# One decode block with its backward pass: K read once, dq from a per-head matrix summed in the forward pass, softmax with keys on partitions, 8 KB rows

## The chip, the cores and the metric

The kernel runs on one core of one Trainium2 chip. The metric is the device time of one execution in microseconds (us), as a median of several executions.

The engines are TensorE (PE; PEld is its weight load), VectorE (DVE), ScalarE (ACT), GpSimd (POOL) and SyncE (SP), each with its own list of instructions, and 16 DMA engines. HBM is the device memory; PSUM is the memory into which the kernel's matmuls write.

## The reference

A decode step: batch 4, one query per sequence, model width 512, 32 heads of 128, 4096 cached keys per head, so 128 pairs of batch and head. The outputs are the step's result and all gradients.

```
q = layernorm(x) @ wq                        # 32 heads of 128
p = softmax(q @ K^T / sqrt(128));  o = p @ V
h = x + o @ wo
h2 = h + (silu(ln(h) @ w1) * (ln(h) @ w3)) @ w2
outputs: h2 and the gradients of x, k_cache, v_cache, wq, wo, w1, w3, w2
```

One cache, K or V, is 134.2 MB in bf16, and so is the gradient of each. Per head, the gradients are two outer products, grad_v = p dO^T and grad_k = dS q^T, with dS = p (dP - c) / sqrt(128), dP = V dO and c = o . dO. The query's gradient is dq = K^T dS.

## The kernel before

It runs the caches in four passes: S = K q and O = V^T p forward; dP = V dO with the grad_v writes; dq = K^T dS with the grad_k writes. So K is read twice and V twice.

```
def load_transposed_half(...):                 # 2048 keys: load, 16 transposes, copies out of PSUM
    dma_eng.dma_start(out=Xh[:], in_=src_rows.rearrange("(p j) d -> p j d", p=P))
    ...
            nc.tensor.transpose(pt[:, i, :], Xh[:, g * GW + i, :], ident_b[:])
        evac_copy(XT[:, g * GW:(g + 1) * GW, :], pt[:], eng=...)
def S_head(b, h, half): ...                    # the query is the weight: all heads' scores in rows
        nc.tensor.matmul(S_ps[QB * b:QB * (b + 1), ...], lhsT=T[...], rhs=KT[...], tile_position=(0, QB * b))
...
for b, h:                                      # last pass: K again
    Kb = kp.tile([P, 2, SJ2, Dh], BF16, ...);  eng.dma_start(out=Kb[:], in_=A_k_cache[b, h]...)
    ... 32 matmuls: dq_ps[...] += T[:, g, ...]^T Kb[:, hh, jj, :]
    nc.vector.tensor_tensor(out=gk[:], in0=dSTall[:, :, bh:bh + 1].to_broadcast([P, SJ, Dh]),
                            in1=rt[:, None, :].to_broadcast([P, SJ, Dh]), op=ALU.mult)
    nc.gpsimd.dma_start(out=out_2[b, h]..., in_=gk...)
...                                            # then, alone at the end: dq transposed, grad of wq, dx
```

## Time and profile before

| | before |
|---|---|
| time, median | 2487.18 us (first 3 runs), 2483.14 us (beside the changed kernel) |
| HBM read / written | 555 / 282 MB |
| forward; MLP; two backward stages; tail | 874; 98; 702 + 718; 48 us |

The main lines stand in the prediction below. One more gives its shape: each place in the row is a fortieth of the span, 62 us, and the digit is the DMA engines' busy share in tenths.

```profile
DMA  9778887888888790799999999997998999999993
```

Read it from left to right: 7 and 8 in the forward stage, a hole at the MLP, 9 through both backward stages, 3 at the tail. The DMA engines bound only the right half. The left half waits for something else.

### The profile page before, as it was taken

How to read it: one execution, taken by the hardware profiler on the slowest of the kernel's cores; microseconds unless marked ns; L12 is line 12 of the kernel's file. 1: busy time of each engine (PE TensorE's matmuls, PEld its weight loads, DVE VectorE, ACT ScalarE, POOL GpSimd, SP SyncE). 2: the span in 40 equal slices, each digit the busy share in tenths (PEclk: the TensorE clock that was granted, in tenths of full speed). 3: DMA queues.
4: the chain of work that ended last, by engine and by line, in shares of the span. 5: the costliest groups of instructions: out<-in, count | busy, mean ns of one | idle time of the engine just before them, and what ended most of it. 6: DMA issues, size and time to landing. Idle time of an engine off the chain costs nothing.

```text
span 2477.8 us, 46386 instructions
## 1 busy us (share of the span) xinstructions
PE 1839.8 (74%) x19974; PEld 1310.2 (53%) x19974; DVE 1503.7 (61%) x1487; ACT 916.8 (37%) x1239; POOL 212.3 (9%) x307
## 2 busy tenths in 40 slices
PE   5999888888888678878777878886655655655655
PEld 3556665655656565455544545553444555554552
DVE  3443323323223104788888898884776888888884
ACT  2443333323233104677776877775321000000001
POOL 1000000000000000111111111111211111111110
PEclk9999999999999897899999999997677777678686
DMA  9778887888888790799999999997998999999993
GB/s 336 233 239 299 329 328 289 336 300 306 298 306 329 288 344 31 307 416 385 386 383 368 391 410 384 386 382 273 382 408 324 401 399 412 398 391 407 415 418 153
DMA packets 222029, 840.47 MB, mean 339 GB/s; under 512 B 17648, under 2 KB 17656, under 8 KB 220800
## 3 DMA queue, kind: packets, MB, share of 16 engines
q1 hardware_dynamic: 92816, 345.87, 37.1%
q0 software_dynamic: 73888, 284.26, 28.3%
q10 hardware_dynamic: 55120, 207.37, 22.8%
q8 instruction: 156, 2.56, 0.4%
q14 instruction: 49, 0.40, 0.0%
HBM read 554.97 MB, written 282.34 MB: 338 GB/s over the span
## 4 chain that ended last, share of the span: by engine, by line
PE 31%; issue 24%; DMA 20%; ACT 17%; DVE 4%; POOL 4%; ACTq 1%; POOLq 0%; DVEq 0%; SPq 0%
ACT XT L155 15%; DMA Vb<-in_A_v_cache_dram 10%; PE pt_tps L205 10%; PE S_ps L285 7%; PE O_ps L351 6%; DMA Xh<-in_A_v_cache_dram 5%; PE dP_ps L630 5%; POOL out_dram L745 3%; DMA Xh<-in_A_k_cache_dram 2%; DMA out_dram<-gk 1%; DVE gk L739 1%; DVE XT L157 1%; PE pt_wT L215 1%; DMA w_sb<-in_B_w_dram 1%; ACTq L200 1%
## 5 line engine op out<-in xcount | busy, mean ns | idle before, releaser
L155 ACT COPY XT<-pt_tps 128x1024 bf16<-128x1024 bf16 x768 | 735.9, 1021 | 694.8 <-PE pt_tps L205 425.3
L205 PE MATMUL pt_tps<-ident_b,Xh 128*128 128x128 bf16 x8192 | 609.5, 221 | 214.0 <-ACT XT L155 91.4
L205 PEld LDWEIGHTS <-Xh 128*128 128x128 bf16 x8192 | 486.2, 98 | 402.5 <-issue 284.5
L739 DVE TENSOR_TENSOR gk<-dSTall,rt 128x4096 bf16<-128x4096 bf16 x128 | 565.9, 4423 | 112.0 <-DMA out_dram<-gk 88.7
L641 DVE TENSOR_TENSOR gv<-PTall,rt 128x4096 bf16<-128x4096 bf16 x128 | 566.3, 4425 | 97.7 <-ACT rt L595 84.8
L729 PE MATMUL dq_ps<-Kb,Tk 128*32 128x128 bf16 x4096 | 365.2, 270 | 220.8 <-DVE Tk L722 220.5
L729 PEld LDWEIGHTS <-Tk 128*32 128x32 bf16 x4096 | 335.4, 124 | 264.1 <-DVE Tk L722 246.7
L351 PE MATMUL O_ps<-Vb,Tp 128*32 128x128 bf16 x4096 | 265.7, 224 | 56.0 <-DMA Vb<-in_A_v_cache_dram 53.0
L157 DVE COPY XT<-pt_tps 128x1024 bf16<-128x1024 bf16 x256 | 177.0, 691 | 188.4 <-PE pt_tps L205 167.4
L285 PE MATMUL S_ps<-XT,Tq 128*32 128x512 bf16 x1024 | 277.9, 386 | 11.2 <-ACT XT L155 9.4
L351 PEld LDWEIGHTS <-Tp 128*32 128x32 bf16 x4096 | 242.5, 100 | 65.1 <-issue 51.1
L595 ACT CAST rt<-rep_ps 128x128 bf16<-128x128 f32 x256 | 73.2, 286 | 536.5 <-DVE gk L739 507.2
L630 PE MATMUL dP_ps<-XT,Td 128*32 128x512 bf16 x1024 | 245.9, 382 | 0.4 <-DVE d_up_rows L157 0.4
L280 DVE COPY Tq<-qT_bf 128x1 bf16<-128x1 bf16 x256 | 39.4, 156 | 274.2 <-PE S_ps L285 273.7
L647 POOL DMA_DIRECT2D out_dram<-gv x128 | 90.3, 706 | 632.8 <-DVE Td L625 550.1
L745 POOL DMA_DIRECT2D out_dram<-gk x128 | 91.6, 716 | 561.2 <-DVE Tk L722 459.9
L630 PEld LDWEIGHTS <-Td 128*32 128x32 bf16 x1024 | 85.9, 96 | 101.3 <-issue 2.1
L285 PEld LDWEIGHTS <-Tq 128*32 128x32 bf16 x1024 | 78.5, 96 | 85.1 <-issue 24.5
L344 DVE COPY Tp<-PTall 128x32 bf16<-128x32 bf16 x128 | 29.3, 242 | 138.4 <-PE O_ps L351 137.4
L432 POOL DMA_DIRECT2D oflat_bf<-O_sb x4 | 2.0, 502 | 805.8 <-ACT O_sb L362 805.8
L593 PEld LDWEIGHTS <-ones_b 1*128 1x128 bf16 x256 | 23.6, 93 | 62.1 <-issue 51.3
L593 PE MATMUL rep_ps<-qflat,ones_b 1*128 1x128 bf16 x128 | 31.9, 249 | 8.7 <-ACT rt L595 8.7
(198 smaller groups left out, 582.4 us busy)
## 6 DMA issues: line engine op xcount, KB each, us to landing
Xh<-in_A_v_cache_dram SPq DMA_DIRECT2D x256, 512.0 KB, 7.0
out_dram<-gv POOLq DMA_DIRECT2D x128, 1024.0 KB, 9.0
out_dram<-gk POOLq DMA_DIRECT2D x128, 1024.0 KB, 10.5
Xh<-in_A_k_cache_dram SPq DMA_DIRECT2D x128, 512.0 KB, 5.9
Vb<-in_A_v_cache_dram ACTq DMA_DIRECT2D x64, 1024.0 KB, 9.0
Vb<-in_A_v_cache_dram SPq DMA_DIRECT2D x64, 1024.0 KB, 9.8
Xh<-in_A_k_cache_dram ACTq DMA_DIRECT2D x128, 512.0 KB, 4.5
Kb<-in_A_k_cache_dram SPq DMA_DIRECT2D x64, 1024.0 KB, 10.0
```

Of the source, the lines that this page charges most:

```text
L155: nc.scalar.copy(out=out_ap, in_=in_ap)
L157: nc.vector.tensor_copy(out=out_ap, in_=in_ap)
L205: nc.tensor.transpose(pt[:, i, :], Xh[:, g * GW + i, :], ident_b[:])
L285: nc.tensor.matmul(S_ps[QB * b:QB * (b + 1), c * SW:(c + 1) * SW], lhsT=T[:, qcol - h:qcol - h + QB], rhs=KT[:, c * SWJ:(c + 1) * SWJ, :], ...
L351: nc.tensor.matmul(O_ps[QB * b:QB * (b + 1), :], lhsT=T[:, g, qcol - h:qcol - h + QB], rhs=Vb[:, hh, jj, :], start=(h == 0 and g == 0), st ...
L595: nc.scalar.copy(out=rt[:], in_=ps[:])
L630: nc.tensor.matmul(dP_ps[QB * b:QB * (b + 1), c * SW:(c + 1) * SW], lhsT=T[:, qcol - h:qcol - h + QB], rhs=VT[:, c * SWJ:(c + 1) * SWJ, :] ...
L641: nc.vector.tensor_tensor(out=gv[:], in0=PTall[:, :, bh:bh + 1].to_broadcast([P, SJ, Dh]), in1=rt[:, None, :].to_broadcast([P, SJ, Dh]), o ...
L647: nc.gpsimd.dma_start(out=out_3[b, h].rearrange("(hh p j) d -> p hh j d", hh=2, p=P), in_=gv.rearrange("p (hh j) d -> p hh j d", hh=2))
L729: nc.tensor.matmul(dq_ps[QB * b:QB * (b + 1), :], lhsT=T[:, g, qcol - h:qcol - h + QB], rhs=Kb[:, hh, jj, :], start=(h == 0 and g == 0), s ...
L739: nc.vector.tensor_tensor(out=gk[:], in0=dSTall[:, :, bh:bh + 1].to_broadcast([P, SJ, Dh]), in1=rt[:, None, :].to_broadcast([P, SJ, Dh]), ...
L745: nc.gpsimd.dma_start(out=out_2[b, h].rearrange("(hh p j) d -> p hh j d", hh=2, p=P), in_=gk.rearrange("p (hh j) d -> p hh j d", hh=2))
```

## The change

Intent: the key dimension stays on the partitions throughout. Then P and dS need no transposing, and forward forms for each head the products PK[k, d] = p[k] K[k, d] and M = sum over k of V[k, :]^T [PK[k, :], p[k]], a 128 x 129 matrix, and kP = sum over k of PK. From these, dq = (M^T dO - c kP) / sqrt(128) without K. The second K pass disappears, one backward loop replaces two, and what stood at the tail moves into that loop. A head's 4096 keys lie 32 to a partition, so rows in DRAM are 8 KB in place of 4 KB. The outer products are written in pairs of elements, so that no operand's innermost step is 0.

The diff, cut to its core:

```
-            nc.tensor.matmul(S_ps[QB * b:QB * (b + 1), ...], lhsT=T[...], rhs=KT[...], ...)
+            for j in range(SJ):
+                nc.tensor.matmul(S_ps[:, hl, j:j + 1], lhsT=KT[:, j, :], rhs=qT_bf[:, bh:bh + 1], start=True, stop=True)
...
+        def softmax(gi):                       # a pair of heads: max, transpose, max, broadcast, exp, sum, 1/sum
+            nc.vector.tensor_reduce(out=mx[:], in_=S_ps[:], axis=AX.X, op=ALU.max)
+            nc.tensor.transpose(xps[0:G, 0:P], mx[:], ident_f[:])
...
+            nc.vector.tensor_tensor(out=P_all[:, gi * G:(gi + 1) * G, :], in0=E[:], in1=rl[...], op=ALU.mult)
+        def M_head(gi, hl):
...
+            nc.vector.tensor_tensor(out=PK[:, :, 0:Dh]..., in0=Kn..., in1=PK[:, :, None, Dh:PKW]..., op=ALU.mult)
+            for j in range(SJ):
+                nc.tensor.matmul(M_ps[:], lhsT=Vn[:, j, :], rhs=PK[:, j, :], start=(j == 0), stop=(j == SJ - 1))
+            for c in range(2):
+                for q in range(4):
+                    nc.tensor.matmul(kP_ps[32 * q:32 * (q + 1), :, :], lhsT=ones_window(w), rhs=PK[:, j0:j0 + 4, 0:Dh], ...)
+            nc.scalar.copy(out=M_all[:, bh, :], in_=M_ps[:, 0:Dh + 1])      # M_all is float32
...
+        for gi in range(NGI + 1):
+            if gi < NGI:
+                for hl in range(G):
+                    S_head(gi, hl)
+                softmax(gi)
+            if gi > 0:
+                for hl in range(G):
+                    M_head(gi - 1, hl)
...
-    (the loop over K that made dq)
+                    nc.tensor.matmul(st_dq["ps"][:, bh:bh + 1], lhsT=M_all[:, bh, 0:Dh], rhs=dOT_f[:, bh:bh + 1], ...)
+            nc.vector.tensor_tensor(out=gv.rearrange("p j (r t) -> p j r t", t=2), in0=P2[...], in1=rdo[...], op=ALU.mult)
+            nc.gpsimd.dma_start(out=rows_of(out_3[b, h]), in_=gv[:])
...
+            nc.vector.tensor_tensor(out=gk.rearrange("p j (r t) -> p j r t", t=2), in0=dS2[...], in1=rq[...], op=ALU.mult)
+            nc.gpsimd.dma_start(out=rows_of(out_2[b, h]), in_=gk[:])
```

## The prediction

The sum came to 833 + 85 + 1052 + 10 = 1980 us, and 1970 was said; the last 10 rested on rates of loads and stores. Two terms of the sum are estimates: 400 GB/s for a saturated mix (the two backward stages of the kernel before had 384 and 388; of the 11 whole fortieths of the last one, ten had 382 to 418), and 2.3 us for each of PK, gv and gk (gv and gk took 4.42 us before). So are the 0.7, 0.4 and 0.8 us for kP, for softmax's small products and for VectorE's small operations. Rival 1 says that the three would cost 4.42 us.

> **What bounds the kernel now.** I read first the table of stretches, cut at the kernel's own stage borders (found in the timeline), then the costliest groups, then the DMA queues, and last the timeline for the price of single instructions.
>
> ```profile
> core 0: us, PE busy (x) PEld busy (x) DVE busy (x) ACT busy (x) POOL busy (x), PEclk, DMA share, GB/s
> 0.00:38.00 38.00, 12.37 (x203) 11.29 (x204) 10.96 (x20) 6.30 (x9) 7.59 (x16) 1.00 0.97 366
> 38.00:912.00 874.00, 739.77 (x9213) 534.19 (x9211) 271.51 (x685) 278.21 (x289) 1.50 (x3) 0.97 0.82 302
> 912.00:1010.00 98.00, 76.41 (x832) 48.92 (x832) 33.86 (x96) 33.67 (x66) 2.02 (x6) 0.74 0.26 92
> 1010.00:1712.00 702.00, 560.69 (x5277) 349.48 (x5277) 587.23 (x390) 508.68 (x641) 93.89 (x130) 0.99 0.99 384
> 1712.00:2430.00 718.00, 426.33 (x4392) 359.57 (x4390) 584.07 (x268) 80.55 (x219) 104.59 (x147) 0.73 0.98 388
> 2430.00:2478.00 48.00, 24.25 (x65) 6.78 (x65) 16.12 (x30) 9.38 (x16) 2.72 (x5) 0.61 0.28 110
> ```
>
> The rows are: start; forward attention (S and O); the MLP and its backward; dP with the grad_v writes; dq with the grad_k writes; tail. The last two columns decide. The two backward stages hold the DMA engines at 98 to 99%: 1420 us are set by **bytes**. The forward stage has a DMA share of 0.82 and 302 GB/s, with PE the busiest engine: it is set by PE's **order and hand-overs** (transpose, copy out of PSUM, matmul). The 98 us of the MLP and the 48 us of the tail are chains of dependent work with the DMA nearly idle.
>
> ```profile
> L155 ACT COPY XT<-pt_tps 128x1024 bf16<-128x1024 bf16 x768 | 735.9, 1021 | 694.8 <-PE pt_tps L205 425.3
> L739 DVE TENSOR_TENSOR gk<-dSTall,rt 128x4096 bf16<-128x4096 bf16 x128 | 565.9, 4423 | 112.0 <-DMA out_dram<-gk 88.7
> L641 DVE TENSOR_TENSOR gv<-PTall,rt 128x4096 bf16<-128x4096 bf16 x128 | 566.3, 4425 | 97.7 <-ACT rt L595 84.8
> L157 DVE COPY XT<-pt_tps 128x1024 bf16<-128x1024 bf16 x256 | 177.0, 691 | 188.4 <-PE pt_tps L205 167.4
> ```
>
> These are the prices of the large elementwise work: 4.42 us for an outer product, 1.02 us (ACT) or 0.69 us (DVE) for a copy of eight transposes. With DVE at 4.42 us in each of two stages, those stages sit just under the DMA bound (587 of 702 us, 584 of 718 us).
>
> ```profile
> q1 hardware_dynamic: 92816, 345.87, 37.1%
> q0 software_dynamic: 73888, 284.26, 28.3%
> q10 hardware_dynamic: 55120, 207.37, 22.8%
> HBM read 554.97 MB, written 282.34 MB: 338 GB/s over the span
> ```
>
> Loads (q1, q10): 345.87 MB in 37.1% of 2477.8 us is 376 GB/s, and q10 gives 367; the stores (q0) give 405. One K or V pass is 134.2 MB: four are read, two written.
>
> ```profile
> 32.20 3.47 PE L228 MATMUL qT_ps<-xhatT,wq_sb 128*128 128x4 bf16 x125 [0.24 <-DVE xhatT L157]
> 409.02 0.38 PE L285 MATMUL S_ps<-XT,Tq 128*32 128x512 bf16 x1
> 409.02 0.39 PE L351 MATMUL O_ps<-Vb,Tp 128*32 128x128 bf16 x4
> 409.24 0.38 PE L285 MATMUL S_ps<-XT,Tq 128*32 128x512 bf16 x1
> ```
>
> The first line: 125 matmuls with full 128x128 weights and four columns in 3.47 us, 28 ns each. The others: S matmuls start 0.22 us apart although four O matmuls for another column group lie between them, so those cost nothing extra.
>
> [...]
>
> **The change part by part.**
>
> *Bytes.* The second K pass goes (-134.2 MB); wo is read once more (+4.2). Left: 425 read + 282 written = 707 MB. Rows grow from 4 KB to 8 KB. A 4 KB packet on a load queue took 16 x 4096 B / 372 GB/s = 176 ns[...]. I use 400 for a saturated mix[...].
>
> *Forward, per head.* Removed: 8 S matmuls of 512 columns (8 x 0.216 = 1.73 us; spacing above), window copies. Kept: 32 transposes (eight in 0.45 us, 56 ns each: 1.8 us). Added: 32 S matmuls of one column (32 x 28 ns = 0.9 us), 32 M matmuls of 130 columns in place of the O ones (about 57 ns: 1.8 us), 8 kP matmuls of 512 columns on four column groups (two rounds of 0.216 together, 1.7 us one by one; the built order breaks them into pieces, so I take 0.7), and softmax's small fp32 matmuls (0.4). Sum: PE 5.6 us a head; before it was 1.8 + 1.73 + 1.8 = 5.3. ACT: 3 copies x 1.02 + exp, M copy: some 3.7. DVE: PK = K*P over 4096 elements written as repeated pairs: [...] 2.3 us[...]; + 0.69 + some 0.8 of small operations = 3.8. DMA: 2.1 MB at 400 GB/s = 5.2. PE and DMA lie close, so the period is PE's work plus hand-overs. In the old steady part (S of a batch beside O of the one before: 96 heads between 196 and 823 us) a head took 6.5 us for 5.3 of work. The new loop has fuller buffers of PE work (S, M and kP of two groups are interleaved in the built order, softmax's steps have 6 to 20 M matmuls between them), so I take **6.2 us**. 128 x 6.2 = 794, + 33 start (wq first; the DMA prefetches meanwhile) + 6 drain = **833 us**, against 912. The old last 90 us, O alone for a batch, are absorbed.
>
> *MLP.* The output projection now accumulates in the forward loop (-7 us, the old attn matmuls), dhh moves ahead; loads of w1 to w3 still start only when forward memory is free. I take **85 us** for 98.
>
> *Backward.* One loop replaces two and the dS transposes between. Per head: 3 MB, 3.146 MB / 400 = 7.9 us. Beside it DVE: gv + gk at 2.3 each + 0.4 = 5.0 us; ACT: 4 copies at 0.94 spacing + replicas 0.3 = 4.1; PE: 1.8 + 0.9 + little = 3. All hidden. With the small gradients and wq, 420.7 MB / 400 = **1052 us**, against 1420.
>
> *Tail.* dq is a matrix product per head with the P-K-V sums, done in the first heads of backward, and dx and grad_wq become jobs inside the loop: 48 us become some **10** of drain.
>
> Sum: 833 + 85 + 1052 + 10 = 1980; I say **1970**[...].
>
> **The rivals.**
> 1. *DVE becomes the bound.* [...] PK, gv and gk cost 4.42 us. Backward would need 2 x 4.42 + 0.4 = 9.3 us a head, 1190 us plus jobs; forward DVE 6.0, about as long as PE. Total some 2150. [...] Chance 1 in 10.
> 2. *Hand-overs of softmax.* S, max, transpose, max, broadcast, exp, sum, reciprocal cross engines about eight times per two heads. If PE stands still for 2 us each time, forward is 7.2 us a head, 960 us, total 2100. For: the old stage lost 1.2 us a head on simpler hand-overs. Against: the interleaving.
> 3. *Buffers too few.* gv and gk have two buffers each; a store landed 9.0 to 10.5 us after issue, plus 2.3 us of filling and about 1 of waiting: 14 us against 15.8 for two heads. It just fits; if landing grows to 14, backward gets 8.5 us a head, +80 us.
> 4. *All better.* Forward DMA-bound: 277 MB / 400 = 692, total 1840.
>
> **Range and chances.** Rivals 1 and 2 give the top, 4 the bottom: 1850 to 2090. Even rivals 1 and 2 together (some 2250) stay under 2487 - 50. Faster 0.97, within 2% 0.02, slower 0.01.
>
> **What would show it.** HBM read about 425 MB. gv, gk, PK at 2.3 us (4.4 would be rival 1). DMA share 0.97 or more in backward at 395 to 410 GB/s; if DVE is busy over 90% there, or its waits for the stores' landing are large, rivals 1 or 3. Forward DMA share about 0.85 at 330 GB/s, PE over 85% busy; PE waiting for nm, exp or mx by over 100 us in total would be rival 2. No stretch of idle DMA at the end. The prediction is wrong if 8 KB rows run below 385 GB/s or forward takes longer than 912 us.

## The result, and the profile after

The changed kernel takes **2204.57 us** (2201.46 to 2205.61, 4 runs), the one before 2483.14 beside it. The ratio is 0.8876 (95% interval 0.8849 to 0.8904). Ratios here are the mean time of one kernel's fast runs over that of the other's of the same rounds, so not quite the ratio of the medians. The direction was right. The time is 235 us above the 1970 predicted and outside the range.

The table of stretches of the kernel after, cut at its own stage borders; the columns are those of the prediction's table. The rows are start, forward, MLP, dq, backward loop, and what is left to store after the last dP.

```profile
0.00:38.00 38.00, 22.86 (x398) 21.20 (x399) 11.94 (x28) 15.53 (x22) 2.68 (x15) 0.93 0.89 360
38.00:944.00 906.00, 791.59 (x13424) 650.62 (x13421) 478.70 (x791) 441.74 (x756) 0.44 (x2) 0.98 0.74 293
944.00:1023.00 79.00, 55.76 (x660) 40.04 (x657) 24.70 (x67) 25.07 (x39) 0.00 (x0) 0.65 0.38 124
1023.00:1086.00 63.00, 62.70 (x328) 61.38 (x325) 7.38 (x10) 5.20 (x8) 2.65 (x5) 0.50 0.19 69
1086.00:2127.00 1041.00, 670.13 (x8695) 548.25 (x8695) 584.73 (x510) 586.00 (x697) 189.22 (x376) 0.59 0.95 376
2127.00:2202.00 75.00, 0.58 (x4) 0.31 (x3) 49.09 (x30) 1.17 (x2) 17.72 (x35) 0.50 0.84 345
```

Set it against the prediction's sum. Forward ends at 944 us where 833 was predicted (+111). The MLP takes 79 (85 predicted, -6). Then come 63 us that the sum doesn't have: TensorE is busy all the time, at half clock, with the DMA engines nearly idle. The backward loop with its end takes 1116 us, where 1052 and 10 were predicted (+54). That makes +222 on the sum of 1980.

The queues and three groups of the kernel after (a group is line, engine, operation, tiles, shapes, count; then busy us and mean ns of one; then the idle time ahead of it and what ended it):

```profile
q1 hardware_dynamic: 66512, 418.94, 49.1%
q0 software_dynamic: 40704, 282.43, 31.5%
HBM read 424.94 MB, written 282.34 MB: 321 GB/s over the span
...
L679 DVE TENSOR_TENSOR gk<-dS,rq 128x4096 bf16<-128x4096 bf16 x128 | 293.2, 2290 | 381.5 <-DMA out_dram<-gk 377.4
L665 DVE TENSOR_TENSOR gv<-P,rdo 128x4096 bf16<-128x4096 bf16 x128 | 292.2, 2283 | 6.9 <-DMA out_dram<-gv 4.7
L288 DVE TENSOR_TENSOR PK<-Kn,PK 128x4096 bf16<-128x4096 bf16 x128 | 293.4, 2292 | 3.8
```

The bytes are as predicted, and the pair layout did what it was meant to: 2.29 us for an outer product that took 4.42 (what in the layout does it, no run shows). VectorE now waits 377 us for stores of gk to land.

The unforeseen 63 us, from the view of one tile (duration in ns as min/median/max, first and last start in us):

```profile
L557 PE MATMUL dq_ps<-dOT_f,M_all x256: 318/352/373, 1023.8 to 1084.5; 128*128 128x1 f32 x128
```

256 records stand for 128 products, two for each float32 product here. All lie between the MLP and the first head of the backward loop.

Last, the hand-over in the forward loop, from the timeline of the kernel after (start, us, engine, line, operation; in brackets the engine's idle time and what ended it):

```profile
425.80 0.98 PE L299 MATMUL M_ps<-PK,Vn 128*128 128x130 bf16 x14
...
426.22 2.29 DVE L288 TENSOR_TENSOR PK<-Kn,PK 128x4096 bf16<-128x4096 bf16 x1
...
428.42 0.17 DVE L318 CAST o<-M_all 128x8 bf16<-128x8 f32 x1
...
428.56 0.59 PE L303 MATMUL kP_ps<-PK,onesw 128*32 128x512 bf16 x1 [1.78 <-DVE PK L288]
...
428.72 2.29 DVE L288 TENSOR_TENSOR PK<-Kn,PK 128x4096 bf16<-128x4096 bf16 x1
428.94 1.06 PE L321 MATMUL at_ps<-wo,o 128*4 128x512 bf16 x2
...
429.93 1.89 PE L183 MATMUL pt_tps<-ident_b,Kn 128*128 128x128 bf16 x16
...
431.06 1.01 ACT L137 COPY KT<-pt_tps 128x1024 bf16<-128x1024 bf16 x1 [3.97 <-PE pt_tps L183]
...
431.86 0.69 DVE L139 COPY KT<-pt_tps 128x1024 bf16<-128x1024 bf16 x1 [0.26 <-PE pt_tps L183]
```

M's products end at 426.7. The next pair's transposes start only at 429.93. Ahead of them in TensorE's order kP's first product waits for PK, and so does, by way of the cast `o` that stands behind the same PK on VectorE, the output projection (at_ps), which only every fourth pair of heads has. In the pairs without it the first 16 transposes go ahead of kP, and the wait follows them (1.54 us at 415.01, 1.48 at 445.40). ScalarE, which copies the transposes out, has stood idle for 3.97 us. And the one copy in four that VectorE makes couldn't have started before 431.0 anyway: it stands behind two PK products of 2.29 us in VectorE's order. (From 428.5 to 432.0 us TensorE had half its clock here; more on this under experiments 7 and 8.)

### The profile page after: what moved, and what is told of

Its sections match the earlier page's. It is cut to its first block, busy times and chain, and to the rows that moved or that the text cites. A ratio compares the mean times of both kernels' runs of the same rounds, so it can differ in the third digit from the quotient of the medians.

```text
span 2202.3 us, 52207 instructions
## 1 busy us (share of the span) xinstructions
PE 1603.6 (73%) x23496; PEld 1321.8 (60%) x23496; DVE 1156.5 (53%) x1431; ACT 1074.7 (49%) x1523; POOL 212.7 (10%) x433
## 3 DMA queue, kind: packets, MB, share of 16 engines
q1 hardware_dynamic: 66512, 418.94, 49.1%
q0 software_dynamic: 40704, 282.43, 31.5%
## 4 chain that ended last, share of the span: by engine, by line
PE 33%; DMA 24%; DVE 17%; issue 15%; ACT 6%; POOL 4%; DVEq 0%; POOLq 0%; SPq 0%; ACTq 0%
DMA out_dram<-gk 20%; PE pt_tps L183 9%; PE M_ps L299 8%; DVE PK L288 6%; DVE gv L665 6%; PE kP_ps L303 4%; PE S_ps L249 4%; ACT KT L137 3%; PE dq_ps L557 2%; DVE gk L679 2%; ACT VT L137 2%; DMA V<-in_A_v_cache_dram 1%; POOL out_dram L671 1%; POOL P L663 1%; DMA out_dram<-gv 1%
## 5 line engine op out<-in xcount | busy, mean ns | idle before, releaser
L137 ACT COPY VT<-pt_tps 128x1024 bf16<-128x1024 bf16 x512 | 494.5, 1020 | 368.6 <-PE dP_ps L661 302.5
L183 PE MATMUL pt_tps<-ident_b,V 128*128 128x128 bf16 x4096 | 457.7, 285 | 147.7 <-ACT VT L137 129.2
L183 PEld LDWEIGHTS <-V 128*128 128x128 bf16 x4096 | 385.5, 131 | 209.3 <-issue 181.7
L137 ACT COPY KT<-pt_tps 128x1024 bf16<-128x1024 bf16 x384 | 376.9, 1014 | 240.5 <-PE pt_tps L183 239.4
L679 DVE TENSOR_TENSOR gk<-dS,rq 128x4096 bf16<-128x4096 bf16 x128 | 293.2, 2290 | 381.5 <-DMA out_dram<-gk 377.4
L183 PE MATMUL pt_tps<-ident_b,Kn 128*128 128x128 bf16 x4096 | 307.5, 225 | 13.4 <-ACT KT L137 9.4
L299 PE MATMUL M_ps<-PK,Vn 128*128 128x130 bf16 x4096 | 305.4, 221 | 3.0 <-DVE PK L287 2.5
L665 DVE TENSOR_TENSOR gv<-P,rdo 128x4096 bf16<-128x4096 bf16 x128 | 292.2, 2283 | 6.9 <-DMA out_dram<-gv 4.7
L288 DVE TENSOR_TENSOR PK<-Kn,PK 128x4096 bf16<-128x4096 bf16 x128 | 293.4, 2292 | 3.8
L299 PEld LDWEIGHTS <-Vn 128*128 128x128 bf16 x4096 | 252.7, 99 | 7.4 <-issue 5.7
L255 DVE TENSOR_REDUCE mx<-S_ps 128x2 f32<-128x64 f32 x64 | 14.4, 225 | 165.1 <-PE S_ps L249 165.1
## 6 DMA issues: line engine op xcount, KB each, us to landing
out_dram<-gk POOLq DMA_DIRECT2D x128, 1024.0 KB, 13.8
```

What stands on the lines that cost most here:

```text
L137: nc.scalar.copy(out=out_ap, in_=in_ap)
L183: nc.tensor.transpose(pt[:, i, :], Xn[:, g * GW + i, :], ident_b[:])
L288: nc.vector.tensor_tensor(out=PK[:, :, 0:Dh].rearrange("p j (r t) -> p j r t", t=2), in0=Kn.rearrange("p j (r t) -> p j r t", t=2), in1=PK ...
L299: nc.tensor.matmul(M_ps[:], lhsT=Vn[:, j, :], rhs=PK[:, j, :], start=(j == 0), stop=(j == SJ - 1))
L665: nc.vector.tensor_tensor(out=gv.rearrange("p j (r t) -> p j r t", t=2), in0=P2[:, :, None, :].to_broadcast([P, SJ, Dh // 2, 2]), in1=rdo[ ...
L679: nc.vector.tensor_tensor(out=gk.rearrange("p j (r t) -> p j r t", t=2), in0=dS2[:, :, None, :].to_broadcast([P, SJ, Dh // 2, 2]), in1=rq[ ...
```

## The experiments

Seventeen kernels ran, three rounds each. The short names in brackets (k1, k4 and so on) are those that the expectations use. A ratio is always to the kernel before of the same call. Where an edit says "wrong", it gives a wrong gradient.

### 1. dq in bf16 (k1)

```
-    M_all = mp.tile([P, NH, Dh + 1], FP32, name="M_all")
+    M_all = mp.tile([P, NH, Dh + 2], BF16, name="M_all")
-    ... lhsT=M_all[:, bh, 0:Dh], rhs=dOT_f[:, bh:bh + 1]
+    ... lhsT=M_all[:, bh, 0:Dh], rhs=dOT_bf[:, bh:bh + 1]
```

> The sums M are kept in bf16 and the 128 dq products run in bf16, nothing else. In the changed kernel they are fp32 and hold PE from 1023 to 1086 us, ahead of the first V transposes, with the DMA at 54 GB/s. Theory 1 (the fp32 burst delays the whole backward): the burst falls from 63 us to under 10, the total by 45 to 60 us to about 2150. Rival (the bytes set the end of backward whatever its start, or V is late anyway): less than 15 us, above 2190.

Measured: correct, 2145.45 us, ratio 0.8639, so 59 us less. The products are now 128 records within 8 us:

```profile
L557 PE MATMUL dq_ps<-dOT_bf,M_all x128: 165/165/211, 1024.7 to 1032.7; 128*128 128x1 bf16 x128
```

The 63 us are the price of float32 here; in bf16 they are about 8. This is the base of most runs below.

### 2. dq's products asked for later (k2)

```
-                if bh >= 1 and jobs:
+                if bh >= 12 and jobs:
```

> fp32 as in the changed kernel, but the jobs with the dq products start at head 12 instead of head 1, so that only 6 of the 128 products stand before the first V transposes. Theory 1 says it is their place that costs, PE having slack later: total down by 40 to 60 us, about 2150. If instead their PE time costs wherever it stands, less than 15 us are won.

Measured: correct, 2200.95 us, ratio 0.8866: no gain. But the trace says that nothing was tried:

```profile
L557 PE MATMUL dq_ps<-dOT_f,M_all x256: 318/352/373, 1025.0 to 1085.7; 128*128 128x1 f32 x128
```

The built order, that is the order in which the built program runs them, put the products back between the MLP and the backward loop. Whether float32 products spread through that loop would have been hidden stays open.

### 3. Rows of 4 KB (k3)

```
-        return ap.rearrange("(p j) d -> p j d", p=P)
+        return ap.rearrange("(hh p j) d -> p hh j d", hh=2, p=P)      # and the tiles in halves
```

> 4 KB rows again for K, V and both gradients (right results). A packet of 4 KB took 159 ns in the kernel before (median), one of 8 KB 309 ns here: 2 x 159 = 318, 3% more. Theory (rows matter by the packet): backward, 1112 us, gets 25 to 35 us longer, forward stays, total about 2235. Rival (rows do not matter): within 10 us of 2204.

Measured: correct, 2202.32 us, ratio 0.8872. The queues of this run:

```profile
q1 hardware_dynamic: 115664, 418.94, 50.2%
q0 software_dynamic: 73472, 282.43, 32.5%
```

Half-size rows hold the engines for 50.2 + 32.5% of 2198.5 us in place of 49.1 + 31.5% of 2202.3. The packets are some 2 to 3% dearer by the byte, and the time doesn't show it. But the backward loop had room for it: it moved 377 GB/s at a DMA share of 0.97, in place of 376 at 0.95. What the rows are worth in a saturated loop isn't tested.

### 4. kP left out, wrong (k4); 5. copies to ScalarE (k11); 6. both, wrong (k16)

Number 4 drops kP's eight products per head from the changed kernel. Number 5 is k1 with

```
-            transpose_blocks(psT, KT, Kn, ["s", "v", "s", "s"])
+            transpose_blocks(psT, KT, Kn, ["s"])
```

Number 6 makes both edits on the changed kernel (float32 dq).

> The kP matmuls are left out (dq, dx and grad of wq wrong on purpose), PK itself stays. In forward they take PE some 0.9 us a head and PE waits some 0.7 us a head for PK in front of them. Theory 2 (PE's order with these waits is the bound of forward): forward falls by 1.3 to 1.6 us a head, 170 to 200 us, to about 760. Rival (the softmax chain or ACT's copies are the bound, the kP work only fills their gaps): less than 80 us.

> Change: dq in bf16 (as k1, 2145 us) and the two of eight K-transpose copies per pair of heads that VectorE did go to ScalarE. Theory now: in the forward loop two waits for the same PK end at nearly the same moment: [...] its K-transpose copies stand behind the two 2.29 us PK products, and TensorE's kP products stand ahead of the next transposes and read PK. Removing one of them leaves the other, as leaving out kP did (2195 for 2204). So this one alone should also give little: 2125 to 2145. Rival (VectorE's copies alone were the hold-up, kP free): 2000 to 2060.

> Change: kP left out (wrong grad of wq on purpose, dq in fp32 as in the changed kernel, 2204 us) and VectorE's K-transpose copies given to ScalarE as well. The two edits that gave 9 us and about 2 us singly. Theory that the two are parallel waits for the same PK products: together they free the next transposes, which then follow M's end; 8 copies at 1.05 us + 4 us of softmax = 12.9 us a pair for 14.2: 2100 to 2135. Rival (the loop is bound by the chain transposes, copies, S, softmax, whatever stands beside it): 2170 or more.

Measured: 4 takes 2195.31 us (0.8849, interval 0.8789 to 0.8910; the changed kernel 0.8876, so the 9 us are not clear of the noise). 5 takes 2143.97, correct (0.864; k1 0.8639). 6 takes 2132.6 (0.8565). Singly they bring 9 and 1 us, together 72. The first theory, that TensorE's own order with kP in it was the bound, expected 4 to gain 170 to 200, and isn't borne out in that size. The theory put in its place is two waits for the same PK, side by side: TensorE's kP products wait for PK ahead of the next transposes, and VectorE's copies of those transposes stand behind PK. Whichever is taken away, the other would end at almost the same moment. The times fit it, but they fit another cause as well:

```profile
20.00:941.00 921.00, 757.00 (x12615) 681.83 (x12614) 483.50 (x799) 458.73 (x767) 0.87 (x4) 0.90 0.74 295
20.00:870.00 850.00, 721.37 (x12615) 640.83 (x12614) 404.40 (x671) 559.09 (x895) 0.87 (x4) 0.98 0.81 319
```

In 4 the granted clock of the stage was 0.90, in 6 it was 0.98 as in the changed kernel. So 4 may have lost to the clock what it won from kP. The next pair was made for that.

### 7. and 8. PK cut off from TensorE, wrong (k9, k22)

```
-    ... rhs=PK[:, j, :]          (M)      rhs=PK[:, j0:j0 + 4, 0:Dh]        (kP)
+    ... rhs=PKc[:, j, :]         (M)      rhs=PKc[:, j0:j0 + 4, 0:Dh]       (kP; PKc is a constant tile)
```

Both on k1; all work of every engine is kept, only TensorE's wait for PK goes. Number 8 also has the copies on ScalarE.

> Change: as k1 (dq in bf16, 2145 us), but M's and kP's products read a constant tile in place of PK; PK is still computed on VectorE (wrong result on purpose, the same work on every engine). TensorE's wait for PK is gone, VectorE's K-transpose copies still stand behind the two PK products. Theory of the two parallel waits: little, 2120 to 2150. Rival (kP's wait was the hold-up, and the run without kP hid its gain in a lower granted clock): 2060 to 2100.

> Change: as the last, and VectorE's K-transpose copies given to ScalarE, so that nothing on the way to the next transposes waits for PK. Theory of the two parallel waits: as in the run without kP and with these copies moved, 65 to 80 us less than k1: 2065 to 2085. Rival (what those two runs gained was kP's own TensorE work): 2120 or more.

Measured: 7 takes 2167.5 us (0.8721), which is 22 us more than k1; 8 takes 2097.08 (0.8429), 48 us less. Forward ends at 957 and at 892 us, against 946 in k1. Again the single removal gains nothing and the double one does, though less than the 65 to 80 expected. And again the single removal ran its forward stage at a low clock (0.92, against 0.99 in 8).

The traces record every change of the granted clock, and they tell how much it hid. In the forward loop it is full except for stretches of 3.4 to 10.2 us at half. The table takes the time from one pair's P to the next pair's, for the 48 intervals without an output projection, and keeps those that had the full clock throughout:

| kernel | us at half clock in the loop | intervals at full clock, of 48 | their mean, us |
|---|---|---|---|
| changed kernel | 41 | 45 | 13.70 |
| 4: no kP | 187 | 25 | 12.48 |
| 6: no kP, copies on ScalarE | 41 | 47 | 12.48 |
| k1 | 51 | 42 | 13.66 |
| 5: copies on ScalarE | 17 | 47 | 13.87 |
| 7: PK cut | 154 | 26 | 12.70 |
| 8: PK cut, copies on ScalarE | 17 | 48 | 12.83 |

At full clock the removal of TensorE's wait for PK alone brings about 1 us a pair, as much as both edits together, and moving the copies alone brings nothing. At one place of every four pairs all 15 intervals of 4 that were compared had the full clock: they take 12.5 us, as in 6, and 13.5 in the changed kernel. What 4 and 7 won there they lost at half clock: they had 146 and 137 us more of it than 6 and 8. In the changed kernel's trace transposes follow each other by 56 ns at full clock and by 107 at half (medians), S's products by 25 and 27. So where TensorE is the bound up to half of the time at half clock is lost, 73 and 68 us (an estimate); 6 and 8 are 63 and 70 us faster. So a second wait of the same length isn't needed to explain these runs.

The moved copies seem to matter by way of the clock. In 4, between 60 and 860 us, TensorE no longer waits for PK (80 us in the changed kernel) but about 29 us for VectorE's copies and 70 for ScalarE's (2 and 11 before), and such pauses go with the half clock. In the traces of the changed kernel and the one before, the shortest time between two changes of the clock is 3.4 us. In eight of these runs (the seven of the table and number 10) the records have 100 half-clock stretches in that window; TensorE was busy for under 0.55 of the 3.4 us before 97 of them, and of 1178 other stretches of 3.4 us only 23 were so little busy. The intervals at full clock are a selection (in 4 nearly all at two places of every four pairs), so this is read from traces and not shown by an experiment; a run with the clock held would show it, and there is none.

### 9. kP asked for one pair later, copies on ScalarE (k12)

```
+            pend.append((bh, PK))
+            if len(pend) > KP_LAG:                # 2
+                kP_head(*pend.pop(0))             # kP's eight products, as before
```

On number 5. PK gets four buffers in place of two.

> Change: as the last, and kP's products issued one pair of heads later, so that neither wait for PK is left in front of the transposes. Theory of the two parallel waits: the next pair's transposes start as soon as M's products end; the loop is then 8 ScalarE copies at 1.03 us plus about 4 us of softmax, 12.3 us a pair for 14.2, so 120 us less than k1's 2145: 2010 to 2050. Rival (each pair is bound by something else, the softmax chain or the copies already): over 2110.

Measured: correct, 2147.73 us, ratio 0.865. A miss, and for the reason of number 2: the built order again put kP right after its PK and ahead of M, and TensorE still waited for it (us in total, times, longest; between 110 and 500 us):

```profile
PE kP_ps L290 <- DVE PK L309: 26.4, 33, 1.5
```

It says nothing against the theory, and nothing for it.

### 10. The softmax of a pair beside the next pair's transposes (k14)

```
+        for gi in range(NGI + 2):
+            for hl in range(G):
+                if gi < NGI:
+                    S_head(gi, hl)
+                if 0 < gi <= NGI:
+                    if hl == 0:
+                        softmax(gi - 1)
+                    PK_head(gi - 1, hl)
+                if gi > 1:
+                    M_head(gi - 2, hl)
```

On k1 with the copies on ScalarE and four PK buffers in place of two. The work is the same, the chain of a pair no longer stands in front of the next.

> Change: as the last, and the softmax of a pair and its PK products moved beside the transposes of the next pair, M's products one pair later still: no chain of a pair stands in front of the next. Same work on each engine. Theory: the forward loop falls to the busiest engine or the bytes, ScalarE 9.9 us, TensorE 10.3 us, loads 4.2 MB at about 400 GB/s 10.5 us a pair, so 10.7 to 11.5 us a pair for 14.2: 180 to 220 us less than k1's 2145: 1925 to 1965. Rival (TensorE's half-clock episodes or hand-overs keep 13 us or more): over 2070.

Measured: correct, **2077.96 us**, ratio 0.8373: 67 us less than k1, where 180 to 220 were expected; the rival's "over 2070" holds. Forward:

```profile
20.00:872.00 852.00, 764.24 (x13669) 655.85 (x13666) 397.31 (x674) 559.74 (x899) 0.87 (x4) 0.99 0.86 318
```

That is 13.3 us per pair of heads (852 / 64) against 14.4 before ((944 - 20) / 64). The chain through softmax and PK was worth about 70 us. About half of it stands in the pairs with the output projection: from P to P they took 16.1 us in k1 and take 13.5 here, the others 13.9 and 13.1. What keeps the loop from the 10.5 us that the bytes alone would take at 400 GB/s (the estimate; the whole fortieths of the changed kernel's backward loop have 344 to 407) isn't shown.

### 11. No maximum in the softmax (k18)

```
-    (mx, its transpose, gm, dg, its broadcast, nm)
-    nc.scalar.activation(out=E[:, hl, :], in_=S_ps[:, hl, :], func=AF.Exp, bias=nm[:, hl:hl + 1], scale=scale, ...)
+    nc.scalar.activation(out=E[:, hl, :], in_=S_ps[:, hl, :], func=AF.Exp, scale=scale, ...)
```

On k1. The scores are small enough here for the result to stay right.

> Change: dq in bf16 (k1, 2145 us), and the maximum of the scores not taken at all: no reduction, transpose, broadcast (the scores here are small, so the result stays right). In the changed kernel's trace the last S product of a pair is 2.0 us ahead of exp; without the maximum about 0.4. Theory that a chain from softmax through PK to the next pair's transposes sets the period: 1.6 us a pair less, 100 us: 2035 to 2060. Rival (TensorE's own work or ScalarE's copies set it): 2115 or more.

Measured: correct, 2116.21 us, ratio 0.8507: 29 us less. That is at the edge of the rival's range (2115 or more), far from the theory's 2035 to 2060: the softmax's own steps are worth less than half of what the reordering in number 10 brought.

### 12. gk's stores from the load queue (k10)

```
-            nc.gpsimd.dma_start(out=rows_of(out_2[b, h]), in_=gk[:])
+            nc.sync.dma_start(out=rows_of(out_2[b, h]), in_=gk[:])
```

On k1. GpSimd issues the stores of both, and VectorE fills the blocks in another order: in the second half of the changed kernel's loop VectorE fills gv, gv, gk, gv, gk, gk for every three heads, and GpSimd issues gv, gv, gk, gk, gv, gk. So a finished block can wait behind an unfinished one: from the end of filling to the issue of the store gk waits 7.1 us (median, in the changed kernel and in k1), gv 0.3.

> Change: as k1, and the stores of gk issued from the queue that issues the V loads, not from GpSimd behind the stores of gv. Theory: the DMA engines stand idle 3 to 4 per cent of the backward stage because finished gk blocks wait behind unfinished gv blocks in one in-order issuer; 20 to 40 us less than k1's 2145: 2105 to 2125. Rival (no gain or a loss, because the loads of V then wait behind gk): 2140 to 2180.

Measured: correct, 2118.85 us, ratio 0.8526: 27 us less. The backward loop and its end, first of k1, then of this run:

```profile
1040.00:2071.00 1031.00, 669.35 (x8662) 550.60 (x8660) 583.29 (x507) 584.87 (x696) 188.86 (x376) 0.59 0.96 378
2071.00:2147.00 76.00, 1.05 (x22) 0.72 (x19) 49.72 (x30) 1.17 (x2) 17.72 (x35) 0.50 0.84 344
```

```profile
1039.00:2114.00 1075.00, 643.22 (x8677) 534.69 (x8675) 636.87 (x535) 591.60 (x697) 169.10 (x280) 0.64 0.96 385
2114.00:2121.00 7.00, 0.00 (x0) 0.00 (x0) 2.48 (x2) 0.00 (x0) 0.00 (x0) 0.57 0.65 266
```

In k1 the reads run ahead and 76 us of stores are left at the end; here 7 us are, and the whole moves faster. A finished gk now waits 0.03 us for its issue. The edit changes two more things: gk's stores move from a software queue (q0) to the hardware queue of the loads (q1), and V's loads take longer from issue to landing (15.1 us in number 15, which makes the same edit, in place of 9.7). So it is not shown that the order alone brings the 27 us.

### 13. Four buffers each for gv and gk (k19)

```
-GO_BUFS = 2
+GO_BUFS = 3                                       # one more joins later, in both; one V buffer less
```

On k1.

> Change: k1 (dq in bf16, 2145 us) with four buffers each for gv and gk in place of three, one V buffer less. Theory: the backward stage runs at 380 GB/s, where the same loop with K read again ran at 419, because VectorE waits for a gk block's store to land before it can fill the next (377 us of such waits in the changed kernel's trace); a fourth buffer takes most of it away: 2085 to 2115. Rival (the order in which GpSimd issues the stores is what empties the queue, a buffer more changes nothing): 2135 to 2155.

Measured: correct, 2142.79 us, ratio 0.8632: nothing. The 377 us that VectorE waits for stores of gk look like too few buffers. With a fourth it waits as long (388 us, 394 in k1), and a finished gk waits 12.2 us for its issue in place of 7.1: the block that the new buffer holds stands in GpSimd's list instead.

### 14. K read once more (k8)

```
+            Kx = v2p.tile([P, SJ, Dh], BF16, name="K2", tag="K2")
+            nc.sync.dma_start(out=Kx[:], in_=rows_of(A_k_cache[b, h]))
```

In the backward loop of the changed kernel, K is loaded and not used (one V buffer less).

> Change: K loaded once more in the backward loop and not used (134 MB more, one V buffer less). What the saved read is worth there: by bytes, 134.2 MB at 385 GB/s = 349 us, so 2204 + 349 = 2553 (2520 to 2590). Rival (the backward stage is not bound by bytes but by stores landing or by VectorE's order, the read is partly hidden): under 2480.

Measured: correct, 2419.45 us, ratio 0.9728: 215 us more, not 349. The backward loop of this run:

```profile
1091.00:2355.00 1264.00, 677.14 (x8670) 571.84 (x8668) 590.43 (x511) 595.51 (x695) 167.66 (x383) 0.57 1.00 417
```

The same loop that moves 376 GB/s in the changed kernel moves 417 when there is more to read. So the bytes don't bind it as tightly as the prediction had it: 107 us of the extra read (134.2 MB / 417 GB/s = 322 us, less the 215 measured) found room in what the loop left unused.

### 15. to 17. Put together (k17, k20, k21)

Number 15 is 10 and 12 together. 16 is 15 with 13's buffers. 17 is 15 with a quarter of the copies back on VectorE.

> Change: the pipelined softmax (k14, 2078 us) together with the stores of gk on the load queue (k10, 27 us less than k1). The two act in different stages, so the sum should hold: 2045 to 2055. Rival (some of the gain of one is the other's, for example a different order of the first backward stores): 2062 or more.

> Change: as k17 (pipelined softmax, gk stores on the load queue, 2050 us), with four buffers each for gv and gk. Theory of the buffers: 10 to 30 us less, 2020 to 2040. Rival of the order (already mended in k17, so buffers add nothing): 2045 to 2055.

> Change: as k17 (2050 us), with VectorE's share of the K-transpose copies given back (one in four). If ScalarE's eight copies a pair of heads bound the pipelined loop (12.9 us a pair, transposes waiting 0.9 us twice for a copy), this gives 20 to 60 us: 1990 to 2030. Rival (VectorE's copies stand behind the PK products again): 2050 to 2120.

Measured, all correct: 15 takes 2050.2 us (0.8242), the sum of its parts, 28 us below number 10. 16 takes **2041.83 us** (0.8231), the lowest median of all but not clear of 15 (intervals 0.8197 to 0.8265 and 0.8211 to 0.8273). 17 takes 2070.66 (0.8343), and forward ends at 895 us in place of 872. The loss stands in the pairs with the output projection (16.6 us from P to P, 13.5 in 15); the others gain (12.6, 13.1 in 15).

## Why the prediction was right or wrong

**Right.** The bytes (425 and 282 MB). The price of the outer products (2.29 us), so rival 1 is out. The tail: the 48 us of dependent work are gone. The MLP within 6 us. Faster, by over 2%.

**Wrong: the sum was 222 us short, in three terms.**

*dq's products: 0 in the sum, 63 us measured.* The prediction's step reads "dq is a matrix product per head with the P-K-V sums, done in the first heads of backward", and prices nothing. It asked where the products go and not what one costs in float32, nor that all 128 come before the first head. Experiment 1 takes the term away: 59 us.

*Forward: "The new loop has fuller buffers of PE work ..., so I take 6.2 us": 7.2 measured* (14.4 us a pair), +111. The pieces were priced well: transposes 56 ns apart, S products 25, M 59, where 56, 28 and 57 stood in the sum. The hand-overs were not. Rival 2 named the size ("7.2 us a head") but looked for it in the softmax's steps: its sign, TensorE waiting over 100 us for them, didn't come (under 30 us), and taking out the maximum brought 29 us. What the list of steps lacked is PK: 4.6 us on VectorE between a pair's softmax and the next pair's transposes. TensorE's kP products wait for it ahead of those transposes (89 us in all); without that wait a pair at full clock takes 12.5 to 12.8 us in place of 13.7 (4 and 6 to 8), but with the copies left on VectorE the time didn't fall, because the clock did. The second thing it lacked is the output projection, booked as a saving ("accumulates in the forward loop (-7 us ...)"): its cast stands behind PK, and every fourth pair takes 16.2 us where the others take 13.7, some 39 us in all (an estimate, 16 x 2.4). A pipelined order took away 67 us of both. The remaining 40 us or so of this term aren't explained.

*Backward: 1052 + 10, 1116 measured*, +54. What failed is that the loop would be saturated ("I use 400 for a saturated mix", "All hidden"): its share is 0.95 at 376 GB/s, and its last 75 us, stores nearly alone, have 0.84 and 345. The price of the bytes held: 0.95 of 1041 us and 0.84 of 75 make some 1052 us of busy DMA engines (an estimate), the very figure of the sum. That it agrees so closely is luck, since the 400 was an estimate whose grounds weren't shown, and the loop moved 376. Rival 3 had "about 1 of waiting" between filling and landing; gk waits 7.1 us for its issue, and landing took 13.8 us where 9.0 to 10.5 had been. So its sign was there, but its cure wasn't: another buffer brings nothing (13; rival 3 counted two, the kernel has a third from early in the loop), issuing gk from the load queue 27 us (12). That the same loop reached 417 GB/s with more reads (14) shows that 376 isn't the limit of the DMA engines. What leaves them idle in the other half of the 54 us stays open.

**The range** took its top, 2090, from rivals 1 and 2, but the prediction's own totals for them are 2150 and 2100. So it held neither of them whole, and had no room for an item left out altogether. The two signs of being wrong that the prediction named both came: under 385 GB/s (376), and forward over 912 us (944).

## What to carry to other kernels

Price every operation that a change adds, the few small ones too, in its data type and at the clock that its stage is granted (the 128 products here took 63 us in float32 and 8 in bf16), and ask the built order where they stand. When removing a wait brings nothing, look for what took the gain before you drop the theory: a second wait, or, as here, the granted clock, stretch by stretch and not as a mean. And check in the trace that the edit moved anything at all, since two of the edits here were undone by the scheduler. A buffer that waits for a store to land may lack not another buffer (nothing here) but another order or queue of issue (27 us here).
